# A scheduler's table of instruction durations, in a fused attention and two-expert kernel

## The chip, the cores and the metric

The kernel runs on one core of a Trainium2 chip. The core has TensorE (PE in the profile; PEld is its weight load), VectorE (DVE), ScalarE (ACT), GpSimd (POOL) and SyncE (SP, which here only issues transfers). The metric is the device time of one execution in microseconds, as the median of several runs. Smaller is better.

## The reference

All tensors are float32 in value; the weights of the two MLPs arrive as float64. Attention runs for 2 batches x 8 heads, 1152 tokens, head dimension 64, with the queries pooled in pairs, so 576 rows of queries per head. Its output, 1152 tokens x 512, goes through two gated MLPs.

```python
q_pool = q.reshape(B, H, S // 2, 2, D).mean(axis=3)
scores = scale * np.matmul(q_pool, k.transpose(0, 1, 3, 2))
attn = np.exp(scores - scores.max(-1)); attn = attn / (attn.sum(-1) + 1e-9)
x = np.matmul(attn, v)                         # then (B*S/2, 512) = (1152, 512)
h = x @ w_in                                   # 512 -> 2048
P = a[0] + a[1]*h + a[2]*h**2 + a[3]*h**3
Q = 1.0 + abs(b[0])*abs(h) + abs(b[1])*h**2
x = (P / (Q + 1e-6)) @ w_out                   # 2048 -> 512
xn = x / sqrt(mean(x*x) + 1e-6) * rms_g
g = xn @ w_gate                                # 512 -> 1536
out = (g * sigmoid(g) * (xn @ w_val)) @ w_out2 # 1536 -> 512
```

## The kernel before

**Three stages.** In the first, attention, two heads make a head pair (8 of them), and the 576 query rows of both heads are cut into 9 tiles of 128 rows, so there are 72 tiles. A tile's scores (L755) fill three PSUM banks called hid; DVE takes the row maximum (L784, tile nm), ACT the exponential (L790, tile p), PE transposes p back into the same banks (L805), and DVE or ACT copies the result into pt (L840, L837). PE then multiplies pt with v (L908, tile av). Tiles go in twos, on two hid buffers: "a pair" below is two such tiles, 36 in all. For each head, kT and qT are made beforehand from kn and qp by PE transposes (L703) and copies out of PSUM (L589 on ACT, L592 on DVE); qp is the sum of the two query rows (L645). At a head pair's end x is copied from av (xt, L589 or L592), divided by the row sums (L959, L964) and split into a high and a low part, x_hi (L592) and x_lo (L605).

In the second stage, the rational MLP, each of 16 units of 128 hidden features is projected by PE (L498 into hid), goes through ten elementwise steps on ACT, DVE and POOL (L1095 to L1146; tiles m_u, m_p, m_q), and ends as g_hi and g_lo. Groups of 2 or 4 units are multiplied with w_out (L498 into accp, two PSUM buffers), and DVE adds each block into acc (L1201). Every product is made of three PE passes: high by high, low by high and high by low part. The third stage is the normalisation and the silu MLP with 12 units (L1353 to L1387, L1416).

**Weights.** A float64 weight is rebuilt as float32 by steps on ACT (L171), DVE (L176, L180, L186) and, for those kept in DRAM for later, ACT again (L211), DVE (L219) and POOL (L215); then it is split into high and low parts (L197, L199, L204, L226, L228, L232). The first 9 weights and the 23 that are kept (far) are done during attention, beside its own work.

**What sets the order.** Nothing about the order is written by hand except PE's own sequence in attention. Every step is an `Op` with an engine, a duration in ns and a key, and `order()` is a list scheduler run while the program is built: it keeps a clock for each engine, takes the step that could start earliest (ties, and in the first stage starts within 80 ns, go to the smaller key), and adds the duration from the table. Some steps have several ways (`op_any`, `W_OTHER`): there the scheduler weighs start plus duration times 1.5 on DVE and ACT (3 on DVE in the last two stages) and takes the lowest. On the chip each engine executes its instructions in just that order, and waits on semaphores where one is not ready. So the table changes no instruction's work; it changes on which engine some run, and in what order they stand.

The durations stand in `S_STEPS`, `W_STEPS` and `W_OTHER` for weights, in `cost()` for all that grows with the width, and with factors at single steps (`copy_ways`, `sub_ways`, `rational`). The steps between PE and the softmax keep durations written at the place (1350 for L784, 1430 for L790).

Of the kernel before, what the change touches and what calls it, by code (L numbers as in the profile page):

```python
# [19 lines left out]
def attention_moe_moe2_kernel(  # L20
# [18 lines left out]
    nc = tc.nc  # L39
# [207 lines left out]
    S_STEPS = [("SP", 1460, w_load)]  # L247
    if wide:
        S_STEPS += [
            ("ACT", 660, w_abs), ("ACT", 660, w_pm), ("DVE", 450, w_shift), ("DVE", 800, w_rest_kept),  # L250
            ("POOL", 1300, w_times),
        ]
    S_STEPS += [("ACT", 660, s_hi), ("POOL", 1450, s_lo), ("SP", 1460, s_store)]


    W_STEPS = [("SP", 1460, w_load)]
    if wide:
        W_STEPS += [("ACT", 500, w_abs), ("DVE", 340, w_shift), ("DVE", 600, w_sign), ("DVE", 600, w_rest)]
    W_STEPS += [("ACT", 500, w_hi), ("POOL", 1230, w_lo)]


    W_OTHER = {
        w_hi: [("POOL", 590, lambda n: w_hi(n, nc.gpsimd)), ("DVE", 340, lambda n: w_hi(n, nc.vector))],
        w_lo: [("DVE", 610, lambda n: w_lo(n, nc.vector))],
        s_hi: [("POOL", 680, lambda n: s_hi(n, nc.gpsimd))],
    }


# [148 lines left out]
    PE, DVE, ACT, POOL = "PE", "DVE", "ACT", "POOL"  # L417

    def cost(eng, n):
        return {PE: 0.425 * n, DVE: 70 + 1.04 * n, ACT: 60 + 0.834 * n, POOL: 148 + 2.104 * n}[eng]  # L420

    wop = {}
    wbuf = {}
# [160 lines left out]
    def copy_ways(dst, src, n, psum=False, scale=None, fast=False, seen=lambda ins: None):  # L584

        by = 1.0 if scale is None else scale

        def on_act():
            seen(nc.scalar.activation(dst(), src(), AF.Copy, scale=by))  # L589

        def on(eng):
            seen(eng.tensor_scalar(dst(), src(), by, 1.0, op0=ALU.mult, op1=ALU.mult))  # L592

        ways = [(ACT, cost(ACT, n), on_act), (DVE, 70 + (0.52 if fast else 1.04) * n, lambda: on(nc.vector))]
        if not psum:
# [7 lines left out]
    def sub_ways(out, a, b, n):  # L603
        def on(eng):
            eng.tensor_sub(out(), a(), b().bitcast(F32))  # L605

        return [(POOL, cost(POOL, n), lambda: on(nc.gpsimd)), (DVE, cost(DVE, n), lambda: on(nc.vector))]

    bank = [[[] for _ in range(3)] for _ in range(2)]
    lo_op, kq_mm = {}, {}  # L610
# [2 lines left out]
    def head_ops(i):  # L613
# [28 lines left out]
        def f_add(eng):  # L642
# [3 lines left out]

        m = NQ * 2 * D
        o_qa = op_any(
            [(POOL, cost(POOL, m), lambda: f_add(nc.gpsimd)), (DVE, cost(DVE, m), lambda: f_add(nc.vector))],
            key, [lq], [bq, bqp],  # L650
        )

# [406 lines left out]
    def rational(u, key):  # L1059
# [19 lines left out]
        def chain(cs):  # L1079
            n = len(cs) * CW  # L1080

            def u_():
                return part("m_u", cs)

            def p_():
                return part("m_p", cs)

            def q_():
                return part("m_q", cs)

# [36 lines left out]

            def f_m_pool():
                nc.gpsimd.tensor_mul(q_(), q_(), u_())

            def f_t():
                stt(p_(), p_(), na0, u_(), op0=ALU.add, op1=ALU.mult)  # L1132

            def f_g():
                stt(p_(), q_(), 2.0, p_(), op0=ALU.subtract, op1=ALU.mult)

            def g_(l):
                if ("g", u) not in env:
                    env["g", u] = [g_tile(x) for x in ("hi", "lo")]
                return env["g", u][l][:, cs[0] * CW:(cs[-1] + 1) * CW]  # L1140

            def f_hi():
                A(g_(0), p_(), AF.Copy)  # L1143

            def f_lo(eng=nc.gpsimd):
                eng.tensor_sub(g_(1), p_(), g_(0).bitcast(F32))  # L1146

            h = [o for c in cs for o in done.get(c, ())]
            o_abs = Op(ACT, cost(ACT, n), k, f_abs, h, [ps, bu])
            o_p1 = Op(ACT, cost(ACT, n) + 150, k + 1000, f_p1, h, [ps, bp])  # L1150
# [345 lines left out]
```

## Time and profile before

| | |
|---|---|
| median of 3 runs | 743.21 us (742.76 to 744.55) |
| the profiled execution's own time | 745.6 us, of which the span is 743.8 |
| PE busy | 699.0 us, 94% |
| DVE busy | 556.3 us, 75% |
| ACT busy | 403.4 us, 54% |
| POOL busy | 280.6 us, 38% |
| mean granted TensorE clock | 0.986 |

Busy time is the time in which at least one instruction of the engine was under way. PE's matmuls are pipelined, so a stretch in which it is busy throughout can still hold slow ones. A row of the timeline gives the start, the length, the engine, the line of the kernel, what is written and read, and in brackets how long the engine had been idle and what ended that.

### The profile page before, as it was taken

Reading aid. Unit: us, or ns where it says so; the run is one execution under the profiler, and the core shown is the slowest. Engines: PE = TensorE matmul, PEld = TensorE weight load, DVE = VectorE, ACT = ScalarE, POOL = GpSimd, SP = SyncE. Lnnn points to the kernel's source line nnn. Section 1 sums busy time; section 2 is a strip of 40 time slices with the busy share of each in tenths; the row PEclk is TensorE's granted clock in tenths of the full one; section 3 lists DMA queues with packets and bytes.
Section 4 is the critical chain, followed back from the end, with each engine's and each line's share of the span. In section 5 each row is a group of like instructions: output and inputs, shape, how many; then the busy total and the mean of one; then the engine's idle time right before and its main releaser. Section 6 shows DMA issues by size and latency. Waiting matters only on the chain.

```text
span 743.8 us, 13108 instructions
## 1 busy us (share of the span) xinstructions
PE 699.0 (94%) x5257; PEld 604.0 (81%) x5257; DVE 556.3 (75%) x723; ACT 403.4 (54%) x633; POOL 280.6 (38%) x245
## 2 busy tenths in 40 slices
PE   8899989998998999899999899899999999999997
PEld 7666666666666668889889799798999899989996
DVE  4799998988878773987977859957769346854844
ACT  4767677677777764898745756416423222312210
POOL 3032455645455520444442352326436123612500
PEclk9999989999999999999999999999999999999999
DMA  7444465446445330223104104000224202420103
GB/s 207 117 155 129 122 214 179 161 162 234 162 150 184 129 115 28 87 85 114 58 16 155 56 1 142 29 28 1 62 82 142 85 29 85 135 93 29 57 1 127
DMA packets 51596, 77.13 MB, mean 104 GB/s; under 512 B 4176, under 2 KB 33872, under 8 KB 51536
## 3 DMA queue, kind: packets, MB, share of 16 engines
q1 hardware_dynamic: 51536, 76.30, 31.6%
q8 instruction: 41, 0.67, 0.4%
q14 instruction: 19, 0.16, 0.1%
HBM read 61.87 MB, written 14.42 MB: 103 GB/s over the span
## 4 chain that ended last, share of the span: by engine, by line
PE 62%; DVE 20%; ACT 9%; issue 6%; POOL 2%; DMA 1%; SPq 0%; DVEq 0%; POOLq 0%; ACTq 0%
PE hid L498 22%; PE accp L498 16%; PE hid L755 9%; PE av L908 8%; PE hid L805 4%; DVE nm L784 2%; DVE pt L840 2%; ACT p L790 2%; DVE m_p L1132 2%; DVE m_q L1111 1%; DVE wc L186 1%; PE prep L703 1%; DVE m_q L1126 1%; ACT m_p L1098 1%; DVE wc L180 1%
## 5 line engine op out<-in xcount | busy, mean ns | idle before, releaser
L498 PE MATMUL hid<-x_hi,win_hi 128*128 128x384 f32 x480 | 162.3, 338 | 5.8 <-issue 2.8
L498 PE MATMUL hid<-x_lo,win_hi 128*128 128x384 f32 x480 | 161.5, 336 | 0.0
L498 PE MATMUL hid<-x_hi,win_lo 128*128 128x384 f32 x480 | 161.2, 336 | 0.0
L790 ACT ACTIVATE p<-hid,nm 128x1152 f32<-128x1152 f32 x72 | 87.7, 1220 | 31.0 <-DVE nm L784 30.5
L755 PE MATMUL hid<-kT,qT 64*128 64x256 f32 (+3 forms) x800 | 99.9, 383 | 3.8 <-DVE pt L840 3.3
L784 DVE TENSOR_REDUCE nm<-hid 128x1 f32<-128x1152 f32 x72 | 94.6, 1351 | 9.6 <-PE hid L755 8.6
L498 PEld LDWEIGHTS hid<-x_hi,win_hi 128*128 128x128 f32 x480 | 90.6, 189 | 8.7 <-issue 5.6
L498 PEld LDWEIGHTS hid<-x_lo,win_hi 128*128 128x128 f32 x480 | 90.6, 189 | 1.2 <-DVE x_lo L1304 0.3
L498 PEld LDWEIGHTS hid<-x_hi,win_lo 128*128 128x128 f32 x480 | 90.7, 189 | 0.0
L755 PEld LDWEIGHTS hid<-kT,qT 64*128 64x128 f32 (+1 forms) x800 | 75.4, 185 | 14.1 <-DVE pt L840 4.7
L805 PEld LDWEIGHTS hid<-ident,p 64*128 64x128 f32 x1296 | 54.3, 143 | 37.4 <-ACT p L790 17.2
L805 PE MATMUL hid<-ident,p 64*128 64x64 f32 x1296 | 69.2, 234 | 12.5 <-ACT p L790 10.1
L1146 POOL TENSOR_TENSOR g_lo<-m_p,g_hi 128x1152 fp32r<-128x1152 f32 (+1 forms) x20 | 47.0, 2360 | 88.0 <-ACT g_hi L1143 88.0
L498 PE MATMUL accp<-g_hi,wout_hi 128*128 128x384 f32 x192 | 66.1, 344 | 11.3 <-DVE acc L1201 9.9
L908 PE MATMUL av<-pt,vn 128*64 128x288 f32 x576 | 76.7, 411 | 0.0
L837 ACT ACTIVATE pt<-hid 128x512 f32<-128x512 f32 (+2 forms) x130 | 55.7, 461 | 31.1 <-PE hid L805 28.4
L199 POOL TENSOR_SCALAR win_hi<-wc 128x512 fp32r<-128x512 f32 x25 | 16.2, 648 | 135.8 <-PE hid L498 105.6
L840 DVE COPY pt<-hid 128x512 f32<-128x512 f32 (+2 forms) x94 | 51.7, 567 | 18.4 <-PE hid L805 18.1
L498 PE MATMUL accp<-g_lo,wout_hi 128*128 128x384 f32 x192 | 64.9, 338 | 0.2 <-POOL g_lo L1146 0.2
L498 PE MATMUL accp<-g_hi,wout_lo 128*128 128x384 f32 x192 | 64.8, 337 | 0.0
L171 ACT ACTIVATE wc<-wraw 128x512 f32<-128x512 f32 x68 | 45.9, 674 | 34.7 <-POOL wout_lo L204 15.8
L908 PEld LDWEIGHTS av<-pt,vn 128*64 128x64 f32 x576 | 38.6, 136 | 26.5 <-issue 1.9
(121 smaller groups left out, 1274.0 us busy)
## 6 DMA issues: line engine op xcount, KB each, us to landing
wraw<-in_moe_w_out_dram SPq DMA_DIRECT2D x28, 512.0 KB, 3.5
far<-spill SPq DMA_DIRECT2D x23, 512.0 KB, 3.5
wraw<-in_moe_w_in_dram SPq DMA_DIRECT2D x16, 512.0 KB, 3.8
wraw<-in_moe_w_gate_dram SPq DMA_DIRECT2D x12, 512.0 KB, 3.5
wraw<-in_moe_w_val_dram SPq DMA_DIRECT2D x12, 512.0 KB, 3.9
kn<-in_k_dram SPq DMA_DIRECT2D x16, 288.0 KB, 3.9
vn<-in_v_dram SPq DMA_DIRECT2D x16, 288.0 KB, 3.8
qn<-in_q_dram SPq DMA_DIRECT2D x16, 256.0 KB, 3.1
```

The costliest lines, as they stand in the source:

```text
L171: nc.scalar.activation(c.bitcast(F32), wt["raw", n][:, :, 1].bitcast(F32), AF.Abs, scale=2.0**-112)
L199: eng.tensor_scalar(hi, w_float(n), 1.0, 1.0, op0=ALU.mult, op1=ALU.mult)
L498: ins = nc.tensor.matmul(dst, lhsT=a[x], rhs=b[y], start=first and i == 0 and p == 0, stop=last and i == n - 1 and p == 2,)
L755: ins = nc.tensor.matmul(ps[to, j, c:c + x1 - x0], lhsT=qT[2 * pr + h][rows, c0:c0 + to.stop - to.start], rhs=kT[2 * pr + h][rows, x0:x1], ...
L784: nc.vector.tensor_reduce(out=e["nm"], in_=scores(), op=ALU.max, axis=AX.X, negate=True)
L790: nc.scalar.activation(e["p"], scores(), AF.Exp, bias=e["nm"], scale=1.0, accum_out=sums[pr][:, t:t + 1])
L805: ins = nc.tensor.transpose(ps[:, g, c:c + 64], e["p"][rows, 128 * j:128 * j + 128], ident[rows, rows])
L837: return nc.scalar.activation(to, src, AF.Copy)
L840: return nc.vector.tensor_copy(to, src)
L908: nc.tensor.matmul(e["av", h][64 * c:64 * c + 64, 0:QW], lhsT=v_tile[2 * pr + h][:, KEYS[kt], :], rhs=pt[pr, h][:, kt, c * QW:(c + 1) * QW ...
L1132: stt(p_(), p_(), na0, u_(), op0=ALU.add, op1=ALU.mult)
L1146: eng.tensor_sub(g_(1), p_(), g_(0).bitcast(F32))
```

## The change

Some thirty numbers of the table are replaced; no step is added, removed or joined to other steps. Most grow: DVE's three steps of a weight from 340, 600 and 600 to 600, 900 and 800, PE's cost per column from 0.425 to 0.45, ACT's fixed part from 60 to 165. Factors are put on single DVE steps. The lines that say most:

```diff
-        W_STEPS += [("ACT", 500, w_abs), ("DVE", 340, w_shift), ("DVE", 600, w_sign), ("DVE", 600, w_rest)]
+        W_STEPS += [("ACT", 680, w_abs), ("DVE", 600, w_shift), ("DVE", 900, w_sign), ("DVE", 800, w_rest)]
...
-        return {PE: 0.425 * n, DVE: 70 + 1.04 * n, ACT: 60 + 0.834 * n, POOL: 148 + 2.104 * n}[eng]
+        return {PE: 0.45 * n, DVE: 100 + 1.09 * n, ACT: 165 + 0.85 * n, POOL: 180 + 2.15 * n}[eng]
...
-            [(POOL, cost(POOL, m), lambda: f_add(nc.gpsimd)), (DVE, cost(DVE, m), lambda: f_add(nc.vector))],
+            [(POOL, cost(POOL, m), lambda: f_add(nc.gpsimd)), (DVE, 1.7 * cost(DVE, m), lambda: f_add(nc.vector))],
```

What this moves between engines, counted over the whole program (before, now): the query sums qp on DVE 6 and 0, on POOL 10 and 16; x_lo on DVE 6 and 3, on POOL 2 and 5; the narrow division L964 on DVE 6 and 0, on POOL 10 and 16; wide copies into kT (128x512) on DVE 8 and 5; wide copies into pt on DVE 67 and 71, on ACT 77 and 73; xt on DVE 26 and 24, on ACT 6 and 8; high parts of kept weights on ACT 5 and 0, on POOL 18 and 23; low parts of weights on DVE 5 and 2, on POOL 40 and 43. In all DVE has 725 instructions and then 708, POOL 250 and then 276. PE's 4553 stay.

The first place is DVE in attention, the eleventh pair of tiles of 36, between its two row maxima and those of the next pair. Here xt, rxh and x are the division at a head pair's end, wc and wraw a weight under way. Before:

```order
L784 TENSOR_REDUCE nm<-hid 128x1 x2
L180 SCALAR_TENSOR_TENSOR wc<-wraw,wc 128x512
L592 TENSOR_SCALAR xt<-av 64x288 x2
L840 COPY pt<-hid 128x8x64
L959 TENSOR_TENSOR xt<-xt,prep 128x512
L964 TENSOR_TENSOR xt<-xt,rxh 64x64 x2
L186 SCALAR_TENSOR_TENSOR wc<-wraw,wc 128x512
L176 TENSOR_SCALAR wc<-wc 128x512
L605 TENSOR_TENSOR x_lo<-xt,x_hi 128x576
L784 TENSOR_REDUCE nm<-hid 128x1 x2
```

The same pair on DVE now:

```order
L784 TENSOR_REDUCE nm<-hid 128x1 x2
L186 SCALAR_TENSOR_TENSOR wc<-wraw,wc 128x512
L176 TENSOR_SCALAR wc<-wc 128x512
L840 COPY pt<-hid 128x8x64
L959 TENSOR_TENSOR xt<-xt,prep 128x512
L219 SCALAR_TENSOR_TENSOR wc<-wraw,wc 128x512
L592 TENSOR_SCALAR x_hi<-xt 128x576
L605 TENSOR_TENSOR x_lo<-xt,x_hi 128x576
L840 COPY pt<-hid 128x128 x2
L784 TENSOR_REDUCE nm<-hid 128x1
L176 TENSOR_SCALAR wc<-wc 128x512
L784 TENSOR_REDUCE nm<-hid 128x1
```

The two xt copies and the two narrow divisions have left DVE (for ACT and POOL), x_hi has come from POOL, and in the next pair a weight step stands between the two maxima.

The second place is ACT in the same pair, from its first exponential (L790; each stands for one tile) to the next pair's. Before:

```order
L790 ACTIVATE p,sums<-hid,nm 128x1152 x2
L837 ACTIVATE pt<-hid 128x8x64
L945 ACTIVATE rxh<-av 128x128
L837 ACTIVATE pt<-hid 128x128
L837 ACTIVATE pt<-hid 128x8x64 x2
L837 ACTIVATE pt<-hid 128x128
L589 ACTIVATE kT_1336<-prep 128x512
L171 ACTIVATE wc<-wraw 128x512
L790 ACTIVATE p,sums<-hid,nm 128x1152 x2
```

ACT there now:

```order
L790 ACTIVATE p,sums<-hid,nm 128x1152
L945 ACTIVATE rxh<-av 128x128
L589 ACTIVATE xt<-av 64x288 x2
L837 ACTIVATE pt<-hid 128x8x64
L790 ACTIVATE p,sums<-hid,nm 128x1152
L171 ACTIVATE wc<-wraw 128x512
L837 ACTIVATE pt<-hid 128x8x64 x2
L211 ACTIVATE wraw<-wraw 128x512
L589 ACTIVATE kT_1349<-prep 128x512
L790 ACTIVATE p,sums<-hid,nm 128x1152
```

The pair's second exponential now stands behind four copies, three of which read av. Over the 36 pairs, copies out of av or prep stand between a pair's two exponentials in 2 pairs before and in 4 now.

The third place is DVE in the rational MLP, units 11 and 12 of 16, where L1132, L1126 and L1135 finish unit 11, L1111 begins unit 12, and L1201 empties an accp buffer for PE. Before:

```order
L1132 SCALAR_TENSOR_TENSOR m_p<-m_p,ncoef,m_u 128x1152
L1126 SCALAR_TENSOR_TENSOR m_q<-m_q,m_u 128x1152
L1111 SCALAR_TENSOR_TENSOR m_q<-m_u,absb,hid 128x1152
L1201 TENSOR_TENSOR acc<-acc,accp 128x384
L1135 SCALAR_TENSOR_TENSOR m_p<-m_q,m_p 128x1152
L1201 TENSOR_TENSOR acc<-acc,accp 128x384
```

There now:

```order
L1126 SCALAR_TENSOR_TENSOR m_q<-m_q,m_u 128x1152
L1132 SCALAR_TENSOR_TENSOR m_p<-m_p,ncoef,m_u 128x1152
L1201 TENSOR_TENSOR acc<-acc,accp 128x384
L1135 SCALAR_TENSOR_TENSOR m_p<-m_q,m_p 128x1152
L1201 TENSOR_TENSOR acc<-acc,accp 128x384
L1111 SCALAR_TENSOR_TENSOR m_q<-m_u,absb,hid 128x1152
```

Unit 12's first step has gone behind two accumulations. At the MLP's end a weight's steps on DVE (L176, L180, L186 before one L1201) are likewise spread out, with an L1201 between them; PE's own order in the last two stages is nearly what it was.

## Rows read from the trace of the kernel before

**Rows 1.** The page, its first lines: busy us (share of the span) and instructions.
```profile
span 743.8 us, 13108 instructions
...
PE 699.0 (94%) x5257; PEld 604.0 (81%) x5257; DVE 556.3 (75%) x723; ACT 403.4 (54%) x633; POOL 280.6 (38%) x245
```

**Rows 2.** Windows, the stages: us, busy PE, PEld, DVE, ACT, POOL; PEclk, DMA, GB/s.
```profile
0.00:285.00 285.00, 263.12 (x2880) 190.88 (x2881) 236.36 (x350) 197.37 (x379) 123.90 (x135) 0.98 0.49 158
285.00:500.00 215.00, 198.13 (x1116) 191.43 (x1115) 167.45 (x169) 136.85 (x154) 77.93 (x37) 0.98 0.21 69
500.00:744.00 244.00, 237.72 (x1265) 221.73 (x1263) 152.45 (x204) 69.21 (x101) 78.77 (x74) 1.00 0.22 71
```

**Rows 3.** Windows, attention: pairs 4 to 16, and pairs 17 to 35.
```profile
31.30:131.72 100.42, 94.70 (x1043) 67.59 (x1041) 94.72 (x144) 71.97 (x137) 44.76 (x47) 0.97 0.50 158
131.72:273.96 142.24, 132.40 (x1510) 93.45 (x1508) 119.72 (x172) 105.48 (x203) 72.39 (x75) 1.00 0.49 168
```

**Rows 4.** Timeline, the first query sums and the first scores.
```profile
5.06 0.83 DVE L645 TENSOR_TENSOR qp<-qn 128x640 f32<-128x640 f32 x1 [3.41 <-DMA qn<-in_q_dram]
...
7.62 1.54 POOL L645 TENSOR_TENSOR qp<-qn 128x640 f32<-128x640 f32 x1 [5.81 <-DMA qn<-in_q_dram]
7.65 2.44 PE L755 MATMUL hid<-kT,qT 64*128 64x256 f32 x20 [0.30 <-DVE qT L592]
```

**Rows 5.** Groups by form, DVE steps that move: busy us, mean ns, idle before.
```profile
L840 DVE COPY pt<-hid 128x512 f32<-128x512 f32 x67 | 45.4, 684 | 13.3 <-PE hid L805 13.0
...
L645 DVE TENSOR_TENSOR qp<-qn 128x640 f32<-128x640 f32 x6 | 6.6, 1092 | 4.2 <-DMA qn<-in_q_dram 3.4 <-issue 0.6 <-PE prep L703 0.2
...
L592 DVE TENSOR_SCALAR kT<-prep 128x512 f32<-128x512 f32 x8 | 5.5, 682 | 0.7 <-PE prep L703 0.6
...
L605 DVE TENSOR_TENSOR x_lo<-xt,x_hi 128x576 fp32r<-128x576 f32 x6 | 4.9, 821 | 0.7 <-POOL x_hi L592 0.6
...
L964 DVE TENSOR_TENSOR xt<-xt,rxh 64x64 f32<-64x64 f32 x6 | 2.0, 326 | 0.0
```

**Rows 6.** Timeline, pairs 11 and 12: ACT, DVE's maxima, PE's wait.
```profile
86.45 1.23 ACT L790 ACTIVATE p<-hid,nm 128x1152 f32<-128x1152 f32 x1
...
87.93 0.60 ACT L837 ACTIVATE pt<-hid 128x512 f32<-128x512 f32 x1 [0.17 <-PE hid L805]
...
92.36 2.61 DVE L784 TENSOR_REDUCE nm<-hid 128x1 f32<-128x1152 f32 x2
...
95.51 1.22 PE L805 MATMUL hid<-ident,p 64*128 64x64 f32 x17 [2.29 <-ACT p L790]
```

**Rows 7.** Windows, the 7.5 us behind that wait; PEclk is third from the end.
```profile
95.00:98.50 3.50, 2.99 (x39) 2.55 (x41) 3.00 (x6) 2.85 (x6) 2.05 (x2) 0.50 0.06 22
98.50:102.50 4.00, 4.00 (x24) 3.37 (x23) 3.94 (x5) 2.41 (x6) 3.23 (x3) 0.58 0.91 303
```

**Rows 8.** Timeline, the first maxima of pairs 5 and 6.
```profile
38.33 1.35 DVE L784 TENSOR_REDUCE nm<-hid 128x1 f32<-128x1152 f32 x1
...
46.35 1.34 DVE L784 TENSOR_REDUCE nm<-hid 128x1 f32<-128x1152 f32 x1
```

**Rows 9.** Timeline, the rational MLP at units 11 and 12.
```profile
421.91 3.83 DVE L1126 SCALAR_TENSOR_TENSOR m_q<-m_q,m_u 128x1152 f32<-128x1152 f32 x1
425.67 1.40 DVE L1111 SCALAR_TENSOR_TENSOR m_q<-m_u,absb,hid 128x1152 f32<-128x1152 f32 x1
...
420.80 3.72 POOL L1146 TENSOR_TENSOR g_lo<-m_p,g_hi 128x1152 fp32r<-128x1152 f32 x1 [5.85 <-ACT g_hi L1143]
...
427.59 0.44 PE L498 MATMUL accp<-g_hi,wout_hi 128*128 128x384 f32 x1 [2.78 <-DVE acc L1201]
```

**Rows 10.** Timeline, the rational MLP's end.
```profile
486.04 3.04 DVE L186 SCALAR_TENSOR_TENSOR wc<-wraw,wc 128x512 uint32<-128x512 uint32 x1
...
489.59 0.44 PE L498 MATMUL accp<-g_hi,wout_hi 128*128 128x384 f32 x1 [1.52 <-DVE acc L1201]
```

**Rows 11.** Timeline, the rational MLP's start: PE at its third unit.
```profile
299.67 0.51 PE L498 MATMUL hid<-x_hi,win_hi 128*128 128x384 f32 x1 [1.98 <-DVE m_p L1104]
```

More of the change, by code (lines that the diff above doesn't have):

```diff
@@ L249, in attention_moe_moe2_kernel @@
         S_STEPS += [
-            ("ACT", 660, w_abs), ("ACT", 660, w_pm), ("DVE", 450, w_shift), ("DVE", 800, w_rest_kept),
-            ("POOL", 1300, w_times),
+            ("ACT", 680, w_abs), ("ACT", 680, w_pm), ("DVE", 540, w_shift), ("DVE", 950, w_rest_kept),
+            ("POOL", 1310, w_times),
         ]
-    S_STEPS += [("ACT", 660, s_hi), ("POOL", 1450, s_lo), ("SP", 1460, s_store)]
+    S_STEPS += [("ACT", 625, s_hi), ("POOL", 1360, s_lo), ("SP", 1460, s_store)]
     W_STEPS = [("SP", 1460, w_load)]
     if wide:
-        W_STEPS += [("ACT", 500, w_abs), ("DVE", 340, w_shift), ("DVE", 600, w_sign), ("DVE", 600, w_rest)]
-    W_STEPS += [("ACT", 500, w_hi), ("POOL", 1230, w_lo)]
+        W_STEPS += [("ACT", 680, w_abs), ("DVE", 600, w_shift), ("DVE", 900, w_sign), ("DVE", 800, w_rest)]
+    W_STEPS += [("ACT", 620, w_hi), ("POOL", 1350, w_lo)]
     W_OTHER = {
-        w_hi: [("POOL", 590, lambda n: w_hi(n, nc.gpsimd)), ("DVE", 340, lambda n: w_hi(n, nc.vector))],
-        w_lo: [("DVE", 610, lambda n: w_lo(n, nc.vector))],
-        s_hi: [("POOL", 680, lambda n: s_hi(n, nc.gpsimd))],
+        w_hi: [("POOL", 730, lambda n: w_hi(n, nc.gpsimd)), ("DVE", 430, lambda n: w_hi(n, nc.vector))],
+        w_lo: [("DVE", 1000, lambda n: w_lo(n, nc.vector))],
+        s_hi: [("POOL", 760, lambda n: s_hi(n, nc.gpsimd))],
     }
@@ L592, in on @@
             seen(eng.tensor_scalar(dst(), src(), by, 1.0, op0=ALU.mult, op1=ALU.mult))
-        ways = [(ACT, cost(ACT, n), on_act), (DVE, 70 + (0.52 if fast else 1.04) * n, lambda: on(nc.vector))]
+        ways = [(ACT, cost(ACT, n), on_act), (DVE, 100 + (0.62 if fast else 1.14) * n, lambda: on(nc.vector))]
         if not psum:
-            ways.append((POOL, 30 + 1.08 * n, lambda: on(nc.gpsimd)))
+            ways.append((POOL, 30 + 1.5 * n, lambda: on(nc.gpsimd)))
         return ways
@@ L605, in on @@
             eng.tensor_sub(out(), a(), b().bitcast(F32))
-        return [(POOL, cost(POOL, n), lambda: on(nc.gpsimd)), (DVE, cost(DVE, n), lambda: on(nc.vector))]
+        return [(POOL, cost(POOL, n), lambda: on(nc.gpsimd)), (DVE, 1.2 * cost(DVE, n), lambda: on(nc.vector))]
     bank = [[[] for _ in range(3)] for _ in range(2)]
@@ L1149, in chain @@
             o_abs = Op(ACT, cost(ACT, n), k, f_abs, h, [ps, bu])
-            o_p1 = Op(ACT, cost(ACT, n) + 150, k + 1000, f_p1, h, [ps, bp])
+            o_p1 = Op(ACT, cost(ACT, n) + 165, k + 1000, f_p1, h, [ps, bp])
             o_p2 = Op(DVE, cost(DVE, n), k + 2200, f_p2, [o_p1], [ps, bp])
@@ L1154, in chain @@
             o_aq = Op(ACT, cost(ACT, n), k + 2000, f_aq, [o_q], [bq])
-            o_ln = Op(ACT, cost(ACT, n) + 130, k + 2000, f_ln, [o_aq], [bq, bu])
-            o_exp = Op(ACT, cost(ACT, n) + 130, k + 8000, f_exp, [o_ln], [bu])
+            o_ln = Op(ACT, cost(ACT, n) + 110, k + 2000, f_ln, [o_aq], [bq, bu])
+            o_exp = Op(ACT, cost(ACT, n) + 110, k + 8000, f_exp, [o_ln], [bu])
             if u in ON_POOL:
-                o_q1 = Op(ACT, cost(ACT, n), k + 9000, f_q1, [o_ln], [bq])
+                o_q1 = Op(ACT, cost(ACT, n) + 100, k + 9000, f_q1, [o_ln], [bq])
                 o_m = Op(POOL, cost(POOL, n), k + 3000, f_m_pool, [o_exp, o_q1], [bq, bu])
             else:
-                o_m = Op(DVE, cost(DVE, n), k + 7000, f_m, [o_exp], [bq, bu])
-            o_t = Op(DVE, cost(DVE, n) + 60, k + 3000, f_t, [o_exp, o_p3], [bp, bu])
-            o_g = Op(DVE, cost(DVE, n), k + 8700, f_g, [o_m, o_t], [bp, bq])
+                o_m = Op(DVE, 1.2 * cost(DVE, n), k + 7000, f_m, [o_exp], [bq, bu])
+            o_t = Op(DVE, 1.3 * cost(DVE, n), k + 3000, f_t, [o_exp, o_p3], [bp, bu])
+            o_g = Op(DVE, 1.3 * cost(DVE, n), k + 8700, f_g, [o_m, o_t], [bp, bq])
             o_hi = Op(ACT, cost(ACT, n), k + 5000, f_hi, [o_g], [bp, *g])
-            o_lo = Op(POOL, cost(POOL, n), k + 5000, f_lo, [o_hi], [bp, *g], [(DVE, cost(DVE, n), lambda: f_lo(nc.vector))])
+            o_lo = Op(POOL, cost(POOL, n), k + 5000, f_lo, [o_hi], [bp, *g], [(DVE, 1.3 * cost(DVE, n), lambda: f_lo(nc.vector))])
             for c in cs:
```

## The prediction

> **What bounds the kernel now.** I read the page's first lines, then the windows by stage, then windows inside attention, and last the waits of PE in the timeline. PE is busy 94% of the 743.8 us span [rows 1], so there are some 45 us without a matmul, and beside them the time that its clock is low. By stage [rows 2]: attention leaves PE idle 21.9 of 285 us, the rational MLP 16.9 of 215, the last stage 6.3 of 244, most of it the tail. What the table can win lies in the first two stages; in the third PE runs nearly without a break, and no order makes its matmuls fewer.
>
> In attention two engines are near their limit. Pairs 4 to 16 last 100.42 us, 7.72 each, with 94.72 / 13 = 7.29 of DVE and 7.28 of PE per pair; pairs 17 to 35 last 142.24 / 19 = 7.49, with 6.30 of DVE and 6.97 of PE [rows 3]. So where DVE carries more, the pair is longer, but far from one for one: 0.23 us of period for 0.99 us of DVE, a slope of 0.24. A late row maximum makes a late exponential, and PE then waits for p. The worst case is at pair 12: its maxima start at 92.36, and PE waits 2.29 us for the exponential at 95.51 [rows 6]. Behind that wait the granted clock is 0.50 and then 0.58 for 7.5 us [rows 7], that is at or near the lower of the two levels, 1.2 GHz; at full clock the same work would have taken about 3.50 x 0.50 + 4.00 x 0.42 = 3.4 us less.
>
> In the rational MLP the waits are single ones behind a blocked DVE: 2.78 us for an accumulation that stood behind a 3.83 us and a 1.40 us step [rows 9], 1.52 us behind a 3.04 us weight step [rows 10], and 1.98 us at the third unit [rows 11].
>
> **The change part by part.** No instruction gets shorter; the table decides engine and order.
>
> *The start.* The first query sum moves from DVE to POOL. It took 0.83 us on DVE and the same form takes 1.54 on POOL [rows 4]; what follows it (transposes, the copy into qT, the scores at 7.65, which waited for qT) is one chain with nothing beside it. Cost 1.54 - 0.83 = +0.7. Between 0.4, if the 0.30 us that the scores waited for qT has other causes, and 1.5, if PE's pause there lowers its clock.
>
> *Attention, DVE's load.* Off DVE go 6 query sums x 1.092 = 6.6 us, 3 x_lo x 0.821 = 2.5, 3 wide kT copies x 0.682 = 2.0 and 6 narrow divisions x 0.326 = 2.0; 4 wide pt copies x 0.684 = 2.7 come [rows 5]. Net 10.3 us lighter; the smaller moves have both signs and are left out. With the slope of [rows 3] that gives 10.3 x 0.24 = 2.5 us. The bounds are 0, if PE hides all of it, and 10.3, if all of it was on the path; I take the slope, since it is the one measurement of how a pair's length follows DVE. POOL gets most of this load; it is busy 123.90 of 285 us [rows 2], so it has room, and what it hands on (the next head's queries, the kept weights) is wanted much later. That cover is gone only at the start, charged above.
>
> *Attention, ACT's order.* In four pairs in place of two, copies now stand between the two exponentials. One of the two old cases is pair 5, from 38.33 to 46.35, 8.02 us [rows 8]; the mean of the 32 pairs of [rows 3] is 242.66 / 32 = 7.58. That is 0.44 for such a pair, two more make +0.9. Between 0, if the maxima are late anyway, and the price of the slow rival below.
>
> *Pairs 11 and 12.* The wait of 2.29 us and the 3.4 us of low clock may both go, because the DVE list ahead of it is shorter; or the new order of ACT makes a like wait one pair earlier. I take 0 net: rows speak for both, and each end is a rival.
>
> *Rational MLP.* At units 11 and 12 the accumulation no longer stands behind unit 12's first step, so it ends that step's 1.40 us earlier and PE's 2.78 becomes about 1.4: -1.4. Unit 12 itself starts later by an accumulation, L1135 and another accumulation, but PE still has two groups of products in front of its next need for it. At the stage's end the three weight steps are spread between accumulations, so only the long one is left in front: PE's wait of 1.52 shrinks to the excess of one blocked step, about 0.4: -1.1. At the stage's start DVE now does the second unit's early steps and a weight ahead of the step that frees hid for PE; that wait was 1.98 and grows by one DVE step of the small form or a weight step, +1.0 as the middle between 0 and 2. Sum -1.5; bounds -6.3 (all three waits gone) and +4.8 (as much again as the first and the last).
>
> *The silu MLP.* PE's order there is nearly the same and it is never short of work; 0, between -0.5 and +2 if a weight comes late.
>
> Sum: +0.7 - 2.5 + 0.9 + 0 - 1.5 + 0 = -2.4 us. Against the profiled execution's own 745.6 us that is 743.2; the median of the runs is 743.21, 2.4 us lower than the profiled one, and the same step from it gives 740.8.
>
> One thing speaks against moving load to POOL. L1126 took 3.83 us from 421.91, over POOL's g_lo of 3.72 from 420.80, and ended 1.2 us after it [rows 9]: it behaved as if it had waited for POOL to end and then run. The Trainium skill, "SBUF — State Buffer", section "Who interferes with whom", says so: a DVE instruction with two SBUF inputs and a GpSimd instruction that reads SBUF use one read port, and whichever comes second is held until the first is done. By that rule, which the trace bears out here, each of the 26 instructions that POOL gains can hold up a DVE step; the sum without it is 740.8, and with it 743.0, as the third rival works it out from the rows alone.
>
> **The rivals.**
>
> *The stall goes with its clock.* If pair 12's maxima come in time, 2.29 + 3.4 = 5.7 us more are saved: 735.1. For it: the list ahead of them loses two xt copies and two divisions. Against it: it still has the division, x_hi and x_lo.
>
> *PE hides it.* If the lighter DVE only waits more for PE, the 2.5 us aren't had: 743.3, no change. For it: pairs 17 to 35, with 1 us less of DVE, still last 7.49, and 6.97 of that is PE. Against it: these pairs were never held up as pair 12 was.
>
> *POOL holds DVE up.* If each of the 6 query sums on POOL blocks a two-input DVE step for its whole 1.54 us, DVE loses 9.2 of the 10.3 us again, and 1.1 x 0.24 = 0.3 us is left: 743.0, no change. For it: the mean of the query sum on DVE is 1.092 while the undisturbed one took 0.83 [rows 4, 5], so such blocking is there today. Against it: a POOL step blocks only what happens to start beside it.
>
> *A late second exponential (slower).* In pair 11 the second exponential began at 86.45. In the new order it stands behind a copy that cannot begin before 87.93, when PE has made its input, and takes 0.60 [rows 6], so it begins at 88.5, 2.1 us later. PE has the other tile's transposes done by then and waits. If that wait lowers the clock as the one at 95.51 did, 3.4 us are added: 740.8 + 5.5 = 746.3; with a second pair of the four like this, 751.8. It decides as soon as DVE's second maximum is in time there, which a lighter DVE makes likelier. Against it: pair 5 had two copies there and cost only 0.44; and a scheduler with truer durations should place copies there only where the maximum is late.
>
> That the table is not what the traces show can also be: the new factor makes L1126 1.2 x (100 + 1.09 x 1152) = 1.63 us, while it took 3.83 beside POOL [rows 9], so one number stands for two cases. It makes a wrong order either way, and I count it with the cases of no change.
>
> **How the numbers follow.** Forecast 740.8 with 0.30 (its own range 737 to 742.5); the stall gone 0.17; PE hides it, or the mean is no better than the old number, 0.15; POOL holds DVE up 0.12; the late exponential at one pair or more 0.26. A difference of 0.3% (2.2 us) is about what this measurement can tell from no change, so "the same" is 741.0 to 745.4. The forecast lies just on its lower side; the first two cases give faster 0.47, the next two the same 0.27, the last slower 0.26. Of the slow case half lies above 748, and of the fast one a third may reach below 731 with the other attention waits gone too: range 731 to 748.
>
> **What would show it.** The first scores at about 8.3 instead of 7.65. DVE busy in attention down from 236 to some 226 us, POOL up by some 20. The pairs at about 7.4 to 7.5 us, and no stretch with a clock near 0.5 at pair 12. At pair 11, PE's wait for the second exponential under 0.5 us; if it is about 2, the slow rival is right. In the rational MLP the wait for the accumulation at unit 12 about 1.4 and the one at the stage's end under 0.5. I am wrong if the last stage, from the first gate product to the end, changes by more than 2 us, or if attention does not get shorter at all while the rational MLP does.

## The result and the profile after

The kernel with the new table takes 738.69 us in the median of 5 runs (735.98 to 739.16), against 743.21 before (742.76 to 744.55). The ratio on record is 0.990, with a 95% interval of 0.9874 to 0.9927: faster, by up to 1%. In us the size is less sure: these two medians differ by 4.5, a ratio of 0.990 is 7.4, and in the later batches of 17 to 23 runs the kernel before had medians of 744.84 to 745.78. The profiled execution itself took 735.98 us, the lowest of the five, and the one before 745.6, above all five. Its page and its windows by stage (us, then busy PE, PEld, DVE, ACT and POOL, the granted clock, the DMA share, GB/s) answer to [rows 1, 2]:

```profile
span 733.9 us, 13104 instructions
...
PE 695.4 (95%) x5257; PEld 602.0 (82%) x5257; DVE 544.3 (74%) x706; ACT 397.3 (54%) x624; POOL 297.6 (41%) x271
```

```profile
0.00:285.00 285.00, 264.81 (x2909) 191.50 (x2911) 227.55 (x336) 193.56 (x373) 143.14 (x156) 0.98 0.49 158
285.00:500.00 215.00, 202.03 (x1144) 197.40 (x1141) 171.98 (x183) 140.88 (x163) 78.89 (x42) 0.98 0.21 69
500.00:734.00 234.00, 228.55 (x1210) 213.13 (x1209) 144.76 (x189) 62.87 (x89) 75.56 (x73) 1.00 0.23 74
```

DVE is lighter in attention by 236.36 - 227.55 = 8.8 us and POOL heavier by 19.2, as the change should make them; PE has 5257 products in both. But PE's share of the first stage hardly moves (263.12 to 264.81); it moves in the second, where PE was idle 16.9 us and is now idle 13.0. Where the two profiled executions part (starts of the same instruction, us):

| stretch | before | after | difference |
|---|---|---|---|
| to the first row maximum | 9.04 | 9.92 | +0.9 |
| pairs 1 to 3 | 22.26 | 20.40 | -1.9 |
| pair 4 to the first MLP product | 248.19 | 245.64 | -2.6 |
| rational MLP, to the norm's first transpose | 227.02 | 221.96 | -5.1 |
| from there to PE's last product | 233.13 | 231.76 | -1.4 |

These sum to -10.0 us, while the medians differ by 4.5. The second row shows why one execution is not enough: over all profiled executions of this study pairs 1 to 3 take between 19.3 and 23.8 us, in two executions of the same order 22.26 and 19.61. The fourth row is no steadier: the old order of the rational MLP takes 227.0 to 229.7 us in three profiled executions, the new one 221.5 to 224.9 in five, where nearly all of the spread arises before the seventh unit.

In attention the waits have moved. These are the pairs 4 to 16 and 17 to 35 after, as in [rows 3]:

```profile
30.32:132.36 102.04, 95.43 (x1051) 67.09 (x1048) 87.54 (x125) 74.62 (x147) 51.94 (x55) 0.97 0.49 154
132.36:270.43 138.07, 131.76 (x1504) 94.50 (x1504) 119.30 (x176) 99.27 (x188) 82.54 (x86) 1.00 0.52 175
```

The first thirteen pairs have 7.2 us less of DVE and are 1.6 us longer; the later nineteen have the same DVE load and are 4.2 us shorter. Pair 11 alone lasts 10.33 us. The timeline there, ACT's second exponential and PE's wait for it (in brackets the idle time and what ended it), and the windows behind it:

```profile
87.44 0.82 ACT L589 ACTIVATE xt<-av 64x288 f32<-64x288 f32 x2
88.29 0.60 ACT L837 ACTIVATE pt<-hid 128x512 f32<-128x512 f32 x1
88.78 1.22 ACT L790 ACTIVATE p<-hid,nm 128x1152 f32<-128x1152 f32 x1
...
90.14 0.78 PE L805 MATMUL hid<-ident,p 64*128 64x64 f32 x18 [2.06 <-ACT p L790]
```

```profile
88.00:92.00 4.00, 1.94 (x33) 1.44 (x34) 3.78 (x5) 3.88 (x8) 2.89 (x3) 0.87 0.60 200
92.00:96.00 4.00, 4.00 (x23) 2.31 (x17) 2.94 (x5) 1.75 (x3) 2.41 (x3) 0.50 0.55 189
```

That is [rows 6, 7] one pair earlier: the stall has changed its place and is not gone. In the rational MLP it is the waits for an emptied accumulator (L1201) that go. What PE waited for there, before and after (us in total, times, longest):

```profile
PE accp L498 <- DVE acc L1201: 9.9, 7, 3.0
PE hid L498 <- issue: 2.8, 2, 1.5
PE hid L498 <- DVE m_p L1104: 2.0, 1, 2.0
PE accp L498 <- ACT acc L1199: 1.5, 2, 1.2
```

```profile
PE hid L498 <- issue: 3.4, 2, 1.8
PE accp L498 <- DVE acc L1201: 3.2, 2, 2.0
PE hid L498 <- DVE m_p L1104: 2.4, 1, 2.4
PE accp L498 <- POOL g_lo L1146: 1.8, 2, 1.1
PE accp L498 <- ACT g_hi L1143: 1.8, 1, 1.8
```

6.7 us of one wait go, and 3.4 us of waits for g_hi and g_lo come, all at the stage's start. Units 11 and 12 are the clearest place, with [rows 9] as what stood there:

```profile
418.88 3.34 DVE L1126 SCALAR_TENSOR_TENSOR m_q<-m_q,m_u 128x1152 f32<-128x1152 f32 x1
422.14 1.41 DVE L1132 SCALAR_TENSOR_TENSOR m_p<-m_p,ncoef,m_u 128x1152 f32<-128x1152 f32 x1
423.47 0.54 DVE L1201 TENSOR_TENSOR acc<-acc,accp 128x384 f32<-128x384 f32 x1
...
418.33 2.67 POOL L1146 TENSOR_TENSOR g_lo<-m_p,g_hi 128x1152 fp32r<-128x1152 f32 x1 [2.94 <-ACT g_hi L1143]
```

The step held up beside POOL still takes 3.34 us, but the accumulation now stands ahead of L1111, and PE does not wait at all.

### The profile page after: what moved, and what is told of

Its sections match the earlier page's. It is cut to its first block, busy times and chain, and to the rows that moved or that the text cites. A ratio compares the mean times of both kernels' runs of the same rounds, so it can differ in the third digit from the quotient of the medians.

```text
span 733.9 us, 13104 instructions
## 1 busy us (share of the span) xinstructions
PE 695.4 (95%) x5257; PEld 602.0 (82%) x5257; DVE 544.3 (74%) x706; ACT 397.3 (54%) x624; POOL 297.6 (41%) x271
## 4 chain that ended last, share of the span: by engine, by line
PE 80%; DVE 9%; ACT 6%; issue 2%; POOL 2%; DMA 1%; SPq 0%; POOLq 0%; DVEq 0%; ACTq 0%
PE hid L498 31%; PE accp L498 22%; PE hid L755 10%; PE av L908 9%; PE hid L805 4%; ACT p L790 2%; DVE pt L840 2%; PE prep L703 2%; DVE nm L784 2%; DVE xt L592 1%; POOL m_q L1129 1%; ACT pt L837 1%; PE prep L955 1%; DVE m_p L1132 1%; DMA qn<-in_q_dram 1%
## 5 line engine op out<-in xcount | busy, mean ns | idle before, releaser
L790 ACT ACTIVATE p<-hid,nm 128x1152 f32<-128x1152 f32 x72 | 87.6, 1219 | 29.5 <-DVE nm L784 29.4
L805 PEld LDWEIGHTS hid<-ident,p 64*128 64x128 f32 x1296 | 52.8, 140 | 37.0 <-ACT p L790 16.0
L805 PE MATMUL hid<-ident,p 64*128 64x64 f32 x1296 | 66.9, 230 | 13.2 <-ACT p L790 10.7
L1146 POOL TENSOR_TENSOR g_lo<-m_p,g_hi 128x1152 fp32r<-128x1152 f32 (+1 forms) x20 | 44.0, 2209 | 70.0 <-ACT g_hi L1143 70.0
L840 DVE COPY pt<-hid 128x512 f32<-128x512 f32 (+1 forms) x102 | 55.5, 564 | 22.2 <-PE hid L805 21.6
L837 ACT ACTIVATE pt<-hid 128x512 f32<-128x512 f32 (+2 forms) x122 | 52.9, 460 | 27.1 <-PE hid L805 26.2
L199 POOL TENSOR_SCALAR win_hi<-wc 128x512 fp32r<-128x512 f32 x26 | 18.1, 698 | 119.8 <-PE hid L498 104.1
```

What stands on the lines that cost most here:

```text
L199: eng.tensor_scalar(hi, w_float(n), 1.0, 1.0, op0=ALU.mult, op1=ALU.mult)
L790: nc.scalar.activation(e["p"], scores(), AF.Exp, bias=e["nm"], scale=1.0, accum_out=sums[pr][:, t:t + 1])
L805: ins = nc.tensor.transpose(ps[:, g, c:c + 64], e["p"][rows, 128 * j:128 * j + 128], ident[rows, rows])
L837: return nc.scalar.activation(to, src, AF.Copy)
L840: return nc.vector.tensor_copy(to, src)
```

## The experiments

In the kernels that mix two orders the table is left aside: the step lists that the scheduler wrote with either table are replayed, one list for attention and one of 1216 steps for the two MLPs, so that pieces of both can be joined. Their diffs are schematic and stand for a list. The ratio is always to the kernel before, with its 95% interval; a difference of two such ratios is uncertain by about 0.0037, or 2.7 us, since most intervals are about ±0.0026; with the old start (±0.0037) and the best pieces (±0.0053) it is 3.4 and 4.4 us. "Over the changed kernel" means over its ratio of 0.990; four kernels with the MLPs wholly in the new order lie at 0.9896 to 0.9923, so each such difference could be up to 1.7 us smaller or 0.3 us larger.

**One stage at a time.**

```diff
 # attention new, MLPs old
+ATTENTION = order by the new table
 MLPS      = order by the old table
```

> Attention in the order that the new table makes, the two MLPs in the order that the old table made; no other difference. My theory, that the gains of the stages are separate and add up: the first product of the rational MLP starts at about 276 us as in the changed kernel (279.5 before), the MLPs take as long as before, so about 3.5 us faster than before in the profile, 0.995. Rival, that the MLPs gain because attention hands over its results and kept weights in better time: most of the whole gain is there, 0.990 to 0.992.

Measured: 744.95 us, 0.9996 (0.9976 to 1.0015).

```diff
 # attention old, MLPs new
 ATTENTION = order by the old table
+MLPS      = order by the new table
```

> The reverse: attention in the old table's order, the two MLPs in the new one's. If the gains add up: first product of the rational MLP at 279.5 us, then some 6 us less than before (5.0 up to the normalisation, 1.4 behind it), 0.992. If the MLPs gain only because of the new attention: within 0.3% of before.

Measured: 738.46 us, 0.9915 (0.9888 to 0.9942). So the gain is the MLPs'. Attention's new order has none that can be told from zero, and both cases of the first expectation (0.995, or 0.990 to 0.992) missed. Yet its stretch from pair 4 to the first MLP product is shorter in every profile (245.6 to 246.2 us in five executions of the new order, 248.2 and 249.0 in two of the old). The later start takes 0.7 of that back; of the 1.3 to 2.7 us that are left, the interval (1.8 us faster to 1.1 slower) has room for a part. The granted clock may hold the rest: its mean is 0.9855 over the 12 runs of the new attention and 0.9887 over the 17 before, which on a span of 743 us is at most 2.4 us of time. Why the clock was lower, no run shows.

**The stall at pair 11: the late exponential taken away.**

```diff
 # ACT in pair 11, the new order
 L790 ACTIVATE p,sums<-hid,nm 128x1152
+L790 ACTIVATE p,sums<-hid,nm 128x1152
 L945 ACTIVATE rxh<-av 128x128
 L589 ACTIVATE xt<-av 64x288 x2
 L837 ACTIVATE pt<-hid 128x8x64
-L790 ACTIVATE p,sums<-hid,nm 128x1152
```

> The changed kernel's order with one step moved: in pair 11 the second exponential stands directly behind the first on ACT, ahead of rxh, the two xt copies and the pt copy. In the changed kernel PE waits 2.06 us for it at 90.1 and its clock is low for about 7 us behind. Theory, that this order is what makes the wait: the wait falls under 0.6 us, the low clock goes with it, pair 11 lasts about 8 us in place of 10.3, and the kernel gains 2 to 5.5 us on the changed one (0.983 to 0.988 of before). Rival, that DVE's division and weight steps behind it are what is late: the wait moves to the next tile and nothing is gained.

Measured: 738.63 us, 0.9923 (0.9894 to 0.9952), no gain over the changed kernel; pair 11 got longer, 11.26 us. The profile shows why. DVE and PE in that pair:

```profile
89.50 0.69 DVE L959 TENSOR_TENSOR xt<-xt,prep 128x512 f32<-128x512 f32 x1 [0.62 <-ACT xt L589]
90.11 1.72 DVE L219 SCALAR_TENSOR_TENSOR wc<-wraw,wc 128x512 uint32<-128x512 uint32 x1
91.75 0.45 DVE L592 TENSOR_SCALAR x_hi<-xt 128x576 fp32r<-128x576 f32 x1
92.23 1.73 DVE L605 TENSOR_TENSOR x_lo<-xt,x_hi 128x576 fp32r<-128x576 f32 x1
93.88 0.47 DVE L840 COPY pt<-hid 128x128 f32<-128x128 f32 x2
```

```profile
88.51 0.78 PE L805 MATMUL hid<-ident,p 64*128 64x64 f32 x17 [0.43 <-ACT p L790]
90.14 0.27 PE L805 MATMUL hid<-ident,p 64*128 64x64 f32 x1 [0.85 <-ACT pt L837]
92.52 0.28 PE L805 MATMUL hid<-ident,p 64*128 64x64 f32 x1 [1.08 <-ACT pt L837]
94.21 0.44 PE L755 MATMUL hid<-kT,qT 64*64 64x128 f32 x4 [1.42 <-DVE pt L840]
```

The rival of the expectation came true. The exponential comes in time (wait 0.43 in place of 2.06), but xt and the pt copies on ACT are later by its length, DVE's division starts 0.7 us later and the last pt copies come behind it: 3.4 us of new waits. So putting the exponential first does not remove the stall: the same pair waits for the next thing that ACT and DVE owe.

**The slope of DVE's load.**

```diff
-        nc.vector.scalar_tensor_tensor(
+        for _ in range(2): nc.vector.scalar_tensor_tensor(
```

This is L219 on the changed kernel, 23 steps in attention, each done twice with the same result.

> The changed kernel's order, but one of DVE's weight steps in attention (L219, 23 times, once a pair from pair 11 on) is done twice, with the same result: some 16 us more of DVE work at 0.68 us each. The prediction's slope of 0.24 us per us of DVE load: attention 3.8 us longer. Rival, PE hides it: under 1 us longer. Rival, DVE is on the path in most pairs: 8 us or more.

Measured: 760.67 us, 1.0217 (1.0185 to 1.0249), some 24 us over the changed kernel by the ratios. The same two stretches:

```profile
30.97:134.31 103.34, 94.77 (x1056) 67.19 (x1052) 91.67 (x132) 74.43 (x147) 51.89 (x55) 0.98 0.50 152
134.31:292.42 158.11, 141.71 (x1499) 102.07 (x1499) 136.50 (x194) 100.10 (x188) 84.42 (x86) 0.92 0.46 153
```

In pairs 4 to 16, 4.1 us more of DVE go with 1.3 us more of time, though the unchanged order itself varies there from 100.8 to 102.6. In pairs 17 to 35, 17.2 us more cost 20.0, and the mean clock there fell from 1.00 to 0.92, which over 158 us is some 12 us of the 20 at most. So the slope of 0.24 is no property of attention: it is 0.3 at one place and 1.2, clock included, at another. What share is DVE's and what the clock's, this run does not separate.

**The first query sum, and ACT's share.**

```diff
 # the changed kernel's order; the first qp back on DVE
-L645 on POOL
+L645 on DVE
```

> The changed kernel's order with the very first query sum on DVE again in place of POOL. The prediction priced its move at +0.7 us; in the changed kernel the first row maximum starts at 9.92 us, before at 9.04. Theory: it starts at about 9.2 and the whole kernel is 0.7 us faster than the changed one. Rival, PE's low clock in the first 24 us eats it: the maximum is earlier, pair 3 starts as late as it did.

Measured: 737.72 us, 0.9896 (0.987 to 0.9923). The first maximum comes at 9.30 in place of 9.44 to 10.09 in the seven profiles that have this sum on POOL and attention's new order. So the start's cost is there, but 0.5 us is below what the timing can tell.

```diff
 # the old order; five high parts of kept weights (s_hi)
-on ACT
+on POOL
```

> The kernel before, with the five high parts of kept weights that stood on ACT (L226, 0.62 us each, in pairs 17 to 28) put on POOL at the same places, as the new table does. In the changed kernel pairs 17 to 35 last 4.2 us less with the same DVE load and 6.2 us less of ACT. If ACT's load is the reason: pairs 17 to 35 get 2 us shorter or more. If the even spread of the weight steps over the pairs is the reason: under 0.5 us.

Measured: 748.08 us, 1.0019 (0.9994 to 1.0043). Pairs 17 to 35 last 143.9 us in its profile, against 142.2 and 143.3 in the old order. So these five steps, 2.9 us of ACT's time there, are not what shortens the nineteen pairs. The other half of the 6.2 us that ACT gets rid of was not moved by itself.

**The table in two halves.**

```diff
 # the weights' steps alone (W_STEPS, S_STEPS, W_OTHER)
-("ACT", 500, w_abs), ("DVE", 340, w_shift), ("DVE", 600, w_sign), ("DVE", 600, w_rest)
+("ACT", 680, w_abs), ("DVE", 600, w_shift), ("DVE", 900, w_sign), ("DVE", 800, w_rest)
```

> The old table with the new durations of the weight steps alone (the three lists of weight steps and their other ways). If the even spread of weight steps makes the gain in pairs 17 to 35, and these durations make the even spread: these pairs last 7.3 us each in place of 7.49 and the attention stage gains 2 us or more. If the general costs of the engines make it: no gain in attention.

Measured: 742.41 us, 0.9958 (0.9937 to 0.9978). Pairs 17 to 35 take 140.8 us, 7.41 each, with 107.1 us of ACT, more than the 105.5 before: a part of the shortening comes with no less of ACT.

```diff
 # all other numbers, the weights' steps as before
-return {PE: 0.425 * n, DVE: 70 + 1.04 * n, ACT: 60 + 0.834 * n, POOL: 148 + 2.104 * n}[eng]
+return {PE: 0.45 * n, DVE: 100 + 1.09 * n, ACT: 165 + 0.85 * n, POOL: 180 + 2.15 * n}[eng]
```

> The reverse: the new general costs and factors, the old durations of the weight steps. If the weight durations make attention's gain: attention as before within 1 us and the rational MLP 3 to 5 us shorter, since its steps' costs are in this part. If the general costs make attention's gain: pairs 17 to 35 at 7.3 us each.

Measured: 738.24 us, 0.990 (0.9877 to 0.9924). The general costs alone give as much as the whole table; the weights' numbers give 0.4% alone and nothing that can be told on top. Pairs 17 to 35 last 7.31 us each, as was expected if the general costs make attention's shorter stretch. With the general costs alone pair 11 lasts 7.66 us, and pair 4 to the first MLP product takes 242.8, the shortest of all.

**The rational MLP in three pieces.** In the changed kernel one piece of the MLPs' list is put back at a time; at both ends of each piece the two orders have done the same steps.

```diff
 # start old
-MLPS[0:192]   by the new table
+MLPS[0:192]   by the old table
```

> The changed kernel; only the start of the rational MLP (its first 192 scheduled steps, about the first three units) is put back into the order of before. Theory A, the new order of that start costs time: from the first MLP product to 340 us PE stood still for 8.2 us after the change against 5.5 before, and the low clock behind it cost 3.4 us against some 3; so the first product to the norm's transposes goes from 222 to 225 us down to some 219 to 221, and the time from 738.7 to about 735. Theory B, of the prediction: the start costs only +1.0, so 737.7. Rival C: the stage is held up by the same steps whatever their order, and what is won at the start is waited for later: 738.7.

Measured: 732.51 us, 0.9819 (0.9782 to 0.9856). From the first MLP product to the norm its profile takes 218.2 us. This is faster than the changed kernel (interval 0.9874 to 0.9927), so the new order of the start costs about 6 us by the timing and 3.8 by these two profiles. The 3.8 is a difference of two single executions, and the start is where executions differ: up to the seventh unit's first product the new start takes 67.9 to 71.3 us in seven profiles (mean 69.5), the old one here 64.6 and, in the best kernel below, 67.3.

```diff
 # middle old
-MLPS[192:438] by the new table
+MLPS[192:438] by the old table
```

> The changed kernel; only the middle of the rational MLP (scheduled steps 192 to 438, about units 4 to 12) is put back into the order of before. Theory A, the gain sits in the accumulations that no longer stand behind a long DVE step in the whole middle: from 340 to 440 us PE stood still 6.6 us before and 1.5 after, so the time goes up by some 5 us, to about 743.5, and the wait of 2.8 us at unit 12 is back. Theory B, of the prediction: only the one wait at units 11 and 12 counts, 1.4 us, so 740.1. Rival C: the middle is hidden, 738.7, and the gain is that of the stage's end and of the last stage.

Measured: 744.63 us, 0.9983 (0.9958 to 1.0009), 6.2 us over the changed kernel. Its profile and the changed kernel's reach the seventh unit at the same time (68.3 us after the first MLP product in both), so what parts them is the middle and what follows it. The middle's waits are back:

```profile
376.52 0.45 PE L498 MATMUL accp<-g_hi,wout_hi 128*128 128x384 f32 x1 [1.37 <-DVE acc L1201]
...
428.24 0.69 PE L498 MATMUL accp<-g_hi,wout_hi 128*128 128x384 f32 x1 [2.79 <-DVE acc L1201]
```

```diff
 # end old
-MLPS[438:588] by the new table
+MLPS[438:588] by the old table
```

> The changed kernel; only the end of the rational MLP (scheduled steps 438 to 588, units 13 to 19 and the weight steps beside them) is put back into the order of before. Theory A: between 460 and 500 us PE stood still 5.2 us before and 3.2 after, and before lost 1.7 us more to a low clock at 470 to 476, so 2 to 4 us are added: 741 to 742.5, with a wait of about 1.5 us for the last weight step back near the end. Theory B, of the prediction: one wait of 1.1 us, 739.8. Rival C: no change, 738.7.

Measured: 740.4 us, 0.9937 (0.9911 to 0.9962), 2.8 us over the changed kernel by the ratios, at the edge of what the timing can tell, and 3.1 by the profiles (225.0 in place of 222.0; here too the start went alike, 68.5 and 68.3 us to the seventh unit). The wait for the last weight step is back:

```profile
476.19 0.44 PE L498 MATMUL accp<-g_hi,wout_hi 128*128 128x384 f32 x1 [1.34 <-DVE acc L1201]
...
484.26 0.45 PE L498 MATMUL accp<-g_hi,wout_hi 128*128 128x384 f32 x1 [1.52 <-DVE acc L1201]
```

**The best pieces together.**

```diff
-ATTENTION = order by the new table
+ATTENTION = order by the new general costs, old weights' steps; first qp on DVE
-MLPS[0:192] by the new table
+MLPS[0:192] by the old table
```

> Attention in the order that the new general costs alone give (with the old numbers for the weights' steps), the first query sum on DVE, the rational MLP's first 192 steps in the order of before, everything else in the order of the change. If the stretches of the profiles add up (attention from the fourth pair to the MLP's first product 242.8 instead of 246.2; the first query sum -0.7; the MLP's start -3 to -4), the time is some 7 us below the changed kernel: 731 to 733. If the start is no gain, 735. If attention's order only moves its waits, 738, as the changed kernel.

Measured: 732.38 us, 0.9813 (0.976 to 0.9865). It beats both kernels, as the one with only the old start does. Its pair 11 lasts 7.65 us, so the stall is gone. But its six runs lie in two groups, and the median and the ratio are taken over both: three at 726.55 to 728.77 us with a mean granted clock of 0.995 to 0.997, three at 736.0 to 736.6 with 0.981. The profiled execution is of the second group; there the clock was low in most of pairs 1 to 3 (23.8 us) and the rational MLP took 220.9 us in place of the 218.2 of the same order above. The first group is below every run with only the old start (730.4 to 734.61), the second above them all. Whether attention's shorter stretch is worth anything in the time stays open.

## Why the prediction came out right, and which of its terms did not

Forecast 740.8, measured 738.69. The time is inside the range and the direction is right, but terms that were wrong in both directions cancelled; that the sum came so near is luck.

- **Start, +0.7: right.** The first maximum came 0.9 us later, and the experiment with the sum on DVE took part of it back. The first scores began at 8.53 where about 8.3 was expected; the sum itself began 0.44 us later than before (5.50 against 5.06), when qn had landed, and that is no matter of the engine.
- **Attention, DVE's load, -2.5: the size nearly fits, the reason fails.** Doubling a DVE step refutes a constant slope, and the load went down in pairs 4 to 16 (which got no shorter) while pairs 17 to 35 got shorter with the same load. The 0.24 was not DVE's even in the kernel before: pairs 11 and 12, with their stall, are in the first group and make most of its excess. These two pairs, before and after:

```profile
83.79:101.12 17.33, 14.70 (x152) 10.89 (x150) 16.48 (x24) 11.79 (x24) 7.68 (x6) 0.82 0.40 119
```

```profile
83.44:102.22 18.78, 15.29 (x152) 10.34 (x150) 14.39 (x21) 13.59 (x27) 10.37 (x11) 0.82 0.45 145
```

Without them the other eleven pairs of the group lasted (100.42 - 17.33) / 11 = 7.55 us before, hardly more than the 7.49 of pairs 17 to 35, and last (102.04 - 18.78) / 11 = 7.57 now, although DVE has 78.24 - 73.15 = 5.1 us less to do in them. PE is busy 80.0 us of them before and 80.1 now. So the slope was mostly the stall, which the sum took up again in a term of its own, and in these eleven pairs PE hides the lighter DVE, as the second rival said. Pairs 17 to 35 are shorter for another reason, which no run settled.
- **ACT's order, +0.9, and pairs 11 and 12, net 0: the mechanism of the slow rival happened, to the number.** The second exponential at 88.78 (worked out: 88.5), a wait of 2.06 us (2.1), and the clock at 0.50 behind it. Pair 12's own wait fell to 0.84 at the same time, so the two exchanged places. The two pairs together went from 17.33 to 18.78 us, +1.45 net where I had 0. The rival's slower time did not come, since the gain elsewhere is larger. What the +0.9 for copies in other pairs is worth, no run separates.
- **Rational MLP, -1.5: mis-sized, the term that decides.** Its three parts, by the profiles (and by the timing): start +3.8 (about +6; single executions range from +0.6 to +6.7), where I had +1.0 and at most +2; units 11 and 12 and the rest of the middle -7.2 (-6.2), where I had -1.4; end -3.1 (-2.8), where I had -1.1. I had taken one wait at units 11 and 12 and left 1.4 of it standing; it went entirely, and waits of 1.35 us at 375.88 and 0.55 at 410.01 went with it. With the same start and the old middle, that accumulation ends 428.19 - 275.08 = 153.1 us after the first MLP product; in the changed kernel it is 424.01 - 275.96 = 148.1. So 5 us are won over the whole middle, and the swap at units 11 and 12 is only its last step. Behind the 2.79 us wait of the old middle the clock was also granted at 0.50 (428 to 430 us), which it was not in the kernel before. The end's long step was the same kind of reading: two other waits for an accumulator ahead of it, 2.98 us at 470.93 and 0.65 at 481.53, weren't in my sum (of all three, 5.2 us, two waits of 2.04 and 1.20 are left in the changed kernel). At the start I priced only the one wait [rows 11], which grew by only 0.4, to 2.39; but the steps moved ahead make the next ones late, and ACT's g_hi then stands behind a step that waits 2.35 us for PE itself:

```profile
314.20 1.22 ACT L1095 ACTIVATE m_u<-hid,absb 128x1152 f32<-128x1152 f32 x1 [2.35 <-PE hid L498]
315.32 1.34 ACT L1143 ACTIVATE g_hi<-m_p 128x384 fp32r<-128x384 f32 x3
...
315.88 0.44 PE L498 MATMUL accp<-g_hi,wout_hi 128*128 128x384 f32 x1 [1.77 <-ACT g_hi L1143]
```

```profile
314.00:318.00 4.00, 1.59 (x5) 1.22 (x5) 2.38 (x3) 3.80 (x6) 2.09 (x3) 0.78 0.40 131
318.00:322.00 4.00, 3.59 (x11) 3.08 (x11) 3.90 (x4) 4.00 (x6) 0.84 (x1) 0.50 0.00 0
```

With the old start PE has a wait of the same length there, 1.76 us at 315.51, this time for an accumulator copy, and the clock stays at 1.00 behind it. But in the best kernel, which has the same MLP order, the same wait of 1.76 us ends at 319.94 and the clock does fall (the first window below is the old start's, the second the best kernel's). So the order does not decide the clock behind this wait, and how much of the start's cost is clock stays open:

```profile
314.00:318.00 4.00, 2.29 (x11) 1.96 (x12) 3.34 (x3) 4.00 (x7) 0.00 (x0) 1.00 0.30 108
```

```profile
320.00:324.00 4.00, 4.00 (x14) 3.61 (x15) 2.54 (x3) 3.26 (x5) 0.00 (x0) 0.60 0.20 51
```

- **Silu MLP, 0: -1.4.** It is the same in every profile of the new order there, 231.75 to 231.79 us in nine, against 233.10 to 233.13 in three of the old; one wait of 0.65 us for an accumulation (at 651.98 before) is gone, and the other 0.7 us was not followed up.
- **POOL holds DVE up: true in single steps, not in the sum.** L1126 ended 1.2 us after POOL's g_lo in both kernels (422.22 and 421.00 here, 425.74 and 424.52 in [rows 9]; the other six of its width take 1.34 to 1.35 us), and L219 in pair 11 took 1.24 us here and 1.72 with the exponential first, beside POOL's L204, against a mean of 0.85 in attention. That is what the Trainium skill, "SBUF — State Buffer", section "Who interferes with whom", says of the shared read port, and the trace agrees. What it costs a whole kernel, no run shows. At units 11 and 12 nobody now waits behind the held step; in pair 11 with the exponential first, PE's wait of 1.42 us for DVE stands behind two that took 1.72 and 1.73.

The wrong-if clause, attention no shorter while the rational MLP is, was met by the timing (0.9996 for attention alone), though in the profiles its stretch from pair 4 on is shorter. So the number was right with the main reason in the wrong stage.

The pieces do not sum exactly: start +6, middle -6.2, end -2.8 and last stage -1.4 give -4.4 us, where the MLPs together gave -6.3. Each is uncertain by 2 to 3 us, so nothing more can be read from that.

## What to carry to other kernels

When a table reorders a whole stage, sum every wait of the engine that bounds it, grouped by what it waited for, rather than the longest one: here one group of seven waits lost 6.7 of its 9.9 us. A slope between two groups of tiles is not a law of the kernel: look first whether a few stalled tiles make it, and test it by adding load before building a sum on it. And when a scheduler's new order is better as a whole, try pieces of the old one: one piece put back was worth nearly as much again as the whole change.

## What was not expected of the hardware

The price of a wait is not fixed. The same order, with the same wait of 1.98 us at the MLP's third unit, was followed by a clock of 0.50 in the kernel before (300 to 302 us), and by 1.00 with only the start's old order put back, where the low stretch came some 10 us later (304.4 to 307.8), among two other waits:

```profile
296.00:298.00 2.00, 2.00 (x14) 2.00 (x13) 1.98 (x4) 2.00 (x5) 1.22 (x1) 1.00 0.00 0
...
306.00:308.00 2.00, 2.00 (x8) 2.00 (x8) 2.00 (x5) 2.00 (x4) 0.00 (x0) 0.56 0.59 172
```

In pairs 1 to 3 too it is the clock that goes with the 3 to 4 us between executions. Over all fourteen profiles of this study the stretch takes 19.3 to 19.6 us where its mean granted clock is 1.00, 20.4 to 20.7 at 0.92, 21.3 and 22.3 at 0.84 and 0.85, 22.4 and 22.7 at 0.77, and 23.8 at 0.71, whichever order the kernel has. In the best kernel's profile it was granted 0.50, the lower level of 1.2 GHz, from 21.3 to 29.3 us, and 1.00 all that time with only the start put back:

```profile
21.30:25.30 4.00, 4.00 (x41) 2.31 (x39) 0.88 (x2) 1.12 (x4) 0.00 (x0) 0.50 0.80 239
25.30:29.30 4.00, 4.00 (x30) 3.08 (x29) 3.00 (x3) 1.75 (x3) 0.00 (x0) 0.50 0.02 8
```

```profile
21.30:25.30 4.00, 3.00 (x35) 2.23 (x33) 3.17 (x3) 2.05 (x4) 0.00 (x0) 1.00 0.80 241
25.30:29.30 4.00, 4.00 (x54) 3.15 (x51) 2.93 (x8) 3.16 (x9) 0.94 (x1) 1.00 0.32 87
```
